# Sliding-window attention with a SwiGLU layer: RMS norm's small steps as tensor_scalar, and a new order table for five engines

## The chip, the cores and the metric

The kernel runs on one core of one Trainium2 chip. The metric is device microseconds for one execution of the whole program. The core has TensorE (PE, matmul, with a separate row PEld for weight loads), VectorE (DVE), ScalarE (ACT), GpSimd (POOL) and SyncE (SP). Plain loads and DMA transposes are issued from SP, loads that cast f32 to bf16 from GpSimd; both run on the same 16 DMA engines.

## What is computed

Attention with a sliding window of 128 and 4 sink keys, then RMS norm and a SwiGLU feed-forward layer, without bias:

```python
# q, k, v: batch 4, heads 8, sequence 768, head_dim 64, f32
scores = q @ k.T / sqrt(64)
keep = (key < 4) | ((0 <= query - key) & (query - key < 128))
a = softmax(where(keep, scores, -1e9))
x = (a @ v) laid out as 3072 tokens x 512
xn = x / sqrt(mean(x * x) + 1e-6) * rms_g
g, val = xn @ w_gate, xn @ w_val          # 512 x 1536 each
out = (g * sigmoid(g) * val) @ w_out      # 1536 x 512, f32 out
```

## The kernel before

The 3072 tokens are 24 blocks of 128 (g = 0 to 23; six blocks are one batch entry), and six groups of four blocks (G = 0 to 5) for the feed-forward part. Per block of attention: q and k are transposed so that head_dim lies on the partitions, by TensorE with a copy by VectorE or ScalarE for blocks 0 to 7 (`pe_t`, `copy_t`), by DMA transposes in SP's queue from block 8 on (`dma_t`). TensorE forms the scores, two heads at a time, with the keys on the partitions; ScalarE takes the exponential into `e`; the masking multiplies or selects `e`: by a bias matmul on TensorE for blocks 0 and 1 (`mask_bias`), by VectorE up to block 15, by GpSimd's affine_select from block 16 on (`tri_pool`, four per block, and `mask_pool_last`, two for the last block of a batch entry). TensorE then forms e times v (`av`, with a column of ones in v that gives the denominator), VectorE divides (`normal`), ScalarE sums the squares (`square`), and VectorE computes the reciprocal root and scales (`rms`).

`rms` is the function that the change edits. It has two tensor_scalar on 128x1 (m, the mean square plus 1e-6; y, a first guess of the reciprocal root from the bits), four scalar_tensor_tensor on 128x1 that refine it (r), and one scalar_tensor_tensor on 128x512 that multiplies x by it and by the gain (xr). xr is then transposed to xnt, by TensorE for blocks 0 to 7 and by DMA in SP's queue from block 8 on.

Per group of the feed-forward part, TensorE multiplies xnt by w_gate and w_val, in pieces whose token width is 128 in group 0, 256 in groups 1 and 2 and 512 after that (g and v, L991); ScalarE takes tanh (th), VectorE makes the silu (p) and the product (hT), TensorE multiplies hT by w_out (o, L1024), ScalarE scales the result to osb and SP stores it.

The kernel first only records its pieces of work with what each needs and gives (`plan.op`; the helpers `dve`, `act`, `pool`, `sp` and `pe` do that). Their order is written out by hand: `ORDER` lists, for each of the five engines, the numbers of the pieces in the order in which this engine does them, counted as they were recorded. Every engine works through its list strictly in order; a piece waits until what it needs is there. `Plan.run` merges the five lists into one program by a small timing model (durations, a DMA model, eight PSUM banks), and the model chooses the banks. Some pieces may run on VectorE or ScalarE; the list in which the number stands decides.

Numbers that matter here: 14, 16 and 18 are the first loads of SP (block 0's k and q as f32, and `grow`, the row of RMS gains); 15 and 17 cast them to bf16; 140 and 138 are the transposes of that k and q on TensorE, 141 and 139 their copies; 20 to 105 are GpSimd's loads, among them 104 (k of block 23) and 105 (v of block 23); 445 to 569 in GpSimd's list are the masks; 564 is the DMA transpose of k of block 23, and 468, 484 and 508 are those of xr of blocks 17, 18 and 19. 106 to 135 are 30 small matmuls on zeros that fill TensorE's time at the start.

GpSimd's loads share one queue. From the ninth on, each load also waits for the landing of the one eight before it.

Of the kernel before, what the change touches and what calls it, by code (L numbers as in the profile page):

```python
# [9 lines left out]
ALU = mybir.AluOpType  # L10
# [24 lines left out]
class Plan:  # L35
# [43 lines left out]
    def run(self, table):  # L79
# [5 lines left out]
        for o in self.ops:  # L85
            for t in o["needs"]:
                users.setdefault(t, []).append(o)
        mode, order = 0, []
        while len(order) < len(self.ops):
            first = None  # L90
            for e in self.START:
                if at[e] == len(ids[e]):
                    continue
                o = self.ops[ids[e][at[e]]]
                k = len(o["takes"])
                if wait[o["at"]] or k > len(self.banks):
                    continue
                ready = o["ready"] + self.HOP[e] if o["ready"] else 0
                if k:
                    ready = max(ready, sorted(self.banks.values())[k - 1] + 40)  # L100
                if o["ring"] == "POOL" and len(last) >= self.DEPTH:
                    ready = max(ready, last[-self.DEPTH])
                start = max(free[e], ready)
                if first is None or start < first[0]:
                    first = start, e, o
            if first is None:
                raise RuntimeError("stuck")
            start, e, o = first
            at[e] += 1
            ns, lat, fn = o["ways"][e]  # L110
            if e == "PE":
                cold = max(0, self.WARM_AT - start)
                ns += min(ns, cold / 2)
                if o["mode"] != mode:
                    ns, mode = ns + 95, o["mode"]
                lat = ns + 180
            for s in o["takes"]:
                i = min(self.banks, key=lambda i: (self.banks[i], i))
                del self.banks[i]
                self.held[s] = i  # L120
            free[e] = start + ns
            end = start + lat
            if o["ring"] is not None:
                end = self.land(o["ring"], end, o["work"]) + self.LATE
                if o["ring"] == "POOL":
                    last.append(end)
            for s in o["drops"]:
                self.banks[self.held[s]] = end + 12
            for t in o["gives"]:
                for x in users.pop(t, ()):  # L130
                    x["ready"] = max(x["ready"], end + 12)
                    wait[x["at"]].discard(t)
            order.append((start, end, e, fn, o))
# [2 lines left out]

ORDER = {
    "PE": """
111 121 124 118 109 135 142 106 140 119 138 134 113 170 108 143 148 136 155 153 129 193
120 172 132 128 162 174 164 175 180 212 195 125 185 117 126 187 115 110 159 122 197 116  # L140
577 166 107 112 131 578 191 204 130 114 133 206 592 597 582 214 593 127 210 583 612 607
587 598 602 588 231 603 216 608 613 617 223 249 225 233 618 235 168 637 647 251 642 229
253 243 632 627 241 260 622 638 266 258 639 633 268 628 294 623 270 643 296 247 644 648
298 264 277 652 279 649 653 662 657 286 288 306 304 654 283 658 672 314 290 667 123 677
663 668 329 678 322 310 682 697 673 344 320 692 683 337 687 335 707 292 359 698 693 717
688 718 350 719 373 352 722 702 366 364 723 712 395 708 703 380 713 382 724 732 727 388
733 728 737 403 742 747 401 729 743 738 734 390 752 748 757 762 753 410 797 758 763 782
425 798 416 418 787 440 777 799 431 772 433 773 767 778 792 768 449 451 788 802 783 803
471 812 804 793 807 813 464 486 808 462 814 480 809 478 822 493 837 823 827 817 838 828
852 842 818 488 502 504 832 847 833 853 843 867 857 848 511 858 872 862 529 873 877 887  # L150
522 863 888 520 878 868 902 540 879 538 889 547 897 903 898 565 937 912 907 913 922 927
908 558 556 892 932 570 882 917 883 918 572 928 923 884 952 942 957 962 947 933 893 943
894 948 938 958 953 977 963 992 959 1002 964 987 997 978 1007 993 982 967 998 983 972
1008 988 968 1012 969 1017 1022 1003 1018 1023 1027 1013 1042 1047 1032 973 1037 1033
1028 974 1038 1048 1043 1039 1049 1044 1052 1055
""",
    "ACT": """
19 15 141 144 146 149 147 145 137 151 150 152 157 173 194 176 178 177 179 181 183 184
182 189 198 200 199 167 201 579 192 208 584 215 211 594 599 589 609 614 232 604 217 219
218 220 619 250 234 227 236-239 252 169 254 256 634 245 624 267 629 640 262 295 273 271  # L160
272 274 297 645 299-302 281 664 650 659 284 308 655 315 316 674 669 317 318 291 330 331
679 332 684 333 345 346 694 347 324 348 699 293 360 689 339 362 709 374 376 720 377 704
354 375 396 397 714 398 399 368 725 739 744 384 749 730 735 759 754 405 764 392 411-414
426-429 420 441 442 779 443 444 774 769 789 784 794 800 435 453 458 460 474 472 473 475
805 466 482 494 495 824 810 496 829 497 819 815 839 834 844 854 849 869 859 506 512-515
530 490 864 531 532 874 533 524 880 904 542 548 890 549-551 899 566 568 909 914 929 924
560 919 934 944 939 574 885 949 954 960 965 979 994 989 984 895 999 1009 1004 1019 1014
1029 1024 970 1034 1040 975 1050 1045 1053 1054
""",
    "DVE": """  # L170
7 0 1 10 2 3 11 12 6 17 139 171 13 156 154 163 158 213 165 196 186 188 160 161 190 4 202
203 205 207 580 209 585 581 586 595 596 600 590 601 610 591 615 605 606 611 221 222 224
226 620 621 228 240 230 616 244 255 257 635 242 261 246 259 630 636 269 625 631 263 275
626 248 276 278 265 280 285 303 282 307 305 287 660 289 665 661 309 670 675 319 671 666
311 323 680 685 681 334 321 676 695 686 338 349 336 325 361 690 696 691 700 351 710 701
363 340 353 705 365 379 378 367 355 715 706 369 389 400 716 711 383 387 740 381 745 385
404 5 402 391 750 746 741 751 760 755 756 406 765 415 761 766 417 419 430 421 432 434
775 776 780 770 781 790 771 452 450 785 795 791 786 436 454 476 796 465 477 463 481 487
479 467 825 485 826 483 830 840 831 841 820 821 503 505 835 489 845 836 855 856 846 850
870 860 861 851 507 875 865 866 521 523 876 871 541 539 525 905 900 901 906 910 543 915  # L180
911 916 559 557 930 571 920 921 925 573 561 931 935 926 940 575 936 945 950 941 955 946
956 951 980 981 995 990 996 985 986 1000 1001 1010 991 1005 1011 1006 1020 1015 1021
1016 1030 1035 1025 1026 1036 1031 1056
""",
    "POOL": """
8 9 20 22 26 21 23 25 29 27 24 32 33 28 36 34 30 35 37 38 42 40 43 41 39 44 31 48 45 47
46 49-53 55 56 58 59 54 57 60-98 445 99 446 447 100 101 459 448 461 102 501 498 103 499
500 516 517 104 518 534 519 536 535 567 537 552 555 105 553 554 569
""",
    "SP": """  # L190
14 18 16 312 327 313 328 646 342 357 343 358 371 641 393 372 394 408 326 656 409 438 341
456 424 651 423 457 439 721 356 370 492 386 491 726 470 469 407 509 422 731 510 437 528
736 801 545 546 484 527 563 468 455 811 508 806 564 544 881 526 562 886 891 576 816 896
971 966 961 1041 976 1046 1051 1057
""",
}

# [2 lines left out]
def kernel(  # L200
# [13 lines left out]
    nc = tc.nc  # L214
# [471 lines left out]
    def rms(g):  # L686
# [7 lines left out]
            scalar2=float(0x5f3759df), op0=ALU.mult, op1=ALU.add,  # L694
        )
        r = small.tile([P, 4], FP32, name="r")
        for o, i0, s, i1, op0 in (
            (0, y, y, m, ALU.mult), (1, r[:, 0:1], -T1, y, ALU.add),
            (2, r[:, 0:1], TP, r[:, 0:1], ALU.add), (3, r[:, 2:3], TQ, r[:, 1:2], ALU.add),
        ):  # L700
            nc.vector.scalar_tensor_tensor(  # L701
                out=r[:, o:o + 1], in0=i0, scalar=s, in1=i1, op0=op0, op1=ALU.mult,
            )
        T["xr", g] = xpool.tile([P, DM], BF16, name="xr")
        nc.vector.scalar_tensor_tensor(  # L705
# [147 lines left out]
    def tri_block(g):  # L853
# [26 lines left out]
        else:  # L880
            for i in range(4):
                pool(590, lambda i=i: tri_pool(g, i), xs + ([("e", g, 0)] if i in (1, 2) else []),
                     [("e", g, i)], g)
            es = [[("e", g, 1), ("e", g, 2)], [("e", g, 0), ("e", g, 3)]]
        T["es", g, 0] = T["es", g, 1] = es

    for g in range(NB):
# [21 lines left out]
        if t + 1 == NT:  # L909
# [8 lines left out]
            for hi in range(2):  # L918
# [5 lines left out]
                        [("e", g, hi)], early)  # L924
                else:
                    pool(590, lambda g=g, hi=hi: mask_pool_last(g, hi), [("x", g, hi)],
                         [("e", g, hi)], g)
                xs.append(("e", g, hi))
            T["xs", g] = [("x", g, 1)]
            T["es", g, 0] = T["es", g, 1] = [xs]  # L930
# [4 lines left out]
        for u in range(2):  # L935
# [12 lines left out]
            early)  # L948
        dve(1745, lambda g=g: rms(g),
            [("ms", g), "gb"] + ([("xt", g - 3)] if g >= 3 else [])  # L950
            + ([("xr", g - 1)] if g else []), [("xr", g)], early)

        G = g // GB
        old = [("F", G - 3, i) for i in range(FTN)] if G >= 3 else []
# [199 lines left out]
```

## Time and profile before

| | |
|---|---|
| median of 3 runs | 245.61 us (244.94 to 246.11) |
| the profiled execution | 246.75 us |
| its span in the profile | 245.0 us |
| TensorE busy | 234.8 us (96%) |
| VectorE busy | 188.3 us (77%) |
| ScalarE busy | 119.4 us (49%) |
| GpSimd busy | 89.7 us (37%) |
| GpSimd's loads | 81760 packets, 13.90 MB |

Times in the profile count from the span's start. A timeline row gives start, duration, engine, line, operation, the tiles written and read, their shapes, how often, and in brackets how long the engine stood idle before it and what ended that. A row of the busy times by stretch gives, after the stretch and its length, the busy microseconds and counts of TensorE, its weight loads, VectorE, ScalarE and GpSimd, then the clock share, the DMA share and GB/s. A row of the waits says which engine and line waited for what, for how long in total, how often, and the longest. Matmuls are pipelined, so a matmul's duration is longer than its distance to the next one.

### The profile page before, as it was taken

The numbers are of one execution on the slowest core, as the hardware profiler recorded it, in microseconds if no ns is written. First come the engines' busy times: TensorE is split into PE (matmuls) and PEld (weight loads), VectorE is DVE, ScalarE is ACT, GpSimd is POOL, SyncE is SP. The second block draws the span as 40 slices with busy tenths as digits, with TensorE's granted clock in tenths as the row PEclk, the third lists the DMA queues.
The fourth block names the chain that finished last, engine by engine and source line by source line (L and its number), as shares of the span: only waits on it lengthen the run. The fifth ranks groups of instructions, "written<-read, shape, count | busy, mean of one in ns | idle before, by whom it ended". The sixth has DMA issues, their size and how long they took to land.

```text
span 245.0 us, 5818 instructions
## 1 busy us (share of the span) xinstructions
PE 234.8 (96%) x2298; PEld 150.5 (61%) x2324; DVE 188.3 (77%) x486; ACT 119.4 (49%) x263; POOL 89.7 (37%) x116
## 2 busy tenths in 40 slices
PE   5899999999999999999999999999989999999994
PEld 2467998875788767687795544445445444444443
DVE  2369889998999999999999889977677853674610
ACT  4377558568575646136765282652732311422221
POOL 8986775679344520039063123052250000000000
PEclk9999999999999999999999999999999999999999
DMA  8999999999999999929995906342033140010305
GB/s 114 164 187 189 181 188 190 153 127 141 149 143 167 128 171 139 207 42 132 199 133 76 190 3 88 86 45 66 3 28 79 21 152 0 0 43 0 131 3 211
DMA packets 113580, 27.38 MB, mean 112 GB/s; under 512 B 103697, under 2 KB 110609, under 8 KB 113554
## 3 DMA queue, kind: packets, MB, share of 16 engines
q0 software_dynamic: 81760, 13.90, 82.6%
q1 hardware_dynamic: 31650, 12.99, 28.4%
q8 instruction: 18, 0.29, 0.5%
q10 hardware_dynamic: 144, 0.13, 0.2%
q14 instruction: 8, 0.07, 0.1%
HBM read 28.31 MB, written 6.29 MB: 141 GB/s over the span
## 4 chain that ended last, share of the span: by engine, by line
PE 83%; DVE 10%; DMA 2%; issue 2%; ACT 1%; SPq 0%
PE v L991 23%; PE o L1024 22%; PE g L991 22%; PE s L601 2%; PE av L659 2%; DMA stage<-in_q_dram 2%; DVE r L701 2%; PE s L523 2%; PE av L654 2%; PE av L644 1%; DVE xr L705 1%; DVE x L673 1%; PE q L483 1%; PE o_last L1042 1%; PE gb L466 1%
## 5 line engine op out<-in xcount | busy, mean ns | idle before, releaser
L991 PE MATMUL v<-xnt,wv 128*128 128x128 bf16 (+2 forms) x525 | 71.6, 282 | 0.4 <-DVE x L673 0.2
L991 PE MATMUL g<-xnt,wg 128*128 128x128 bf16 (+2 forms) x522 | 70.9, 281 | 0.6 <-DVE hT L1014 0.2
L1024 PE MATMUL o<-wo,hT 128*128 128x512 bf16 x259 | 65.4, 379 | 1.8 <-DVE p L1004 0.8
L998 ACT ACTIVATE th<-g 128x512 bf16<-128x512 f32 x72 | 41.1, 600 | 47.3 <-PE g L991 46.6
L1004 DVE SCALAR_TENSOR_TENSOR p<-th,g 128x512 bf16<-128x512 bf16 x72 | 48.0, 681 | 14.3 <-ACT th L998 13.9
L1014 DVE TENSOR_TENSOR hT<-p,v 128x512 bf16<-128x512 bf16 x72 | 47.8, 682 | 11.3 <-PE v L991 10.3
L991 PEld LDWEIGHTS <-wv 128*128 128x128 bf16 x528 | 43.3, 98 | 20.5 <-issue 0.4
L991 PEld LDWEIGHTS <-wg 128*128 128x128 bf16 x528 | 42.8, 98 | 19.6 <-issue 0.5
L1024 PEld LDWEIGHTS <-hT 128*128 128x128 bf16 x276 | 25.4, 98 | 26.8 <-issue 1.5
L395 POOL DMA_DIRECT2D v<-in_v_dram x24 | 21.4, 893 | 28.6 <-DVE rden L672 19.0
L610 ACT ACTIVATE e<-s 128x384 bf16<-128x384 f32 x52 | 22.6, 495 | 8.1 <-PE s L601 6.4
L681 ACT ACTIVATE sq<-x 128x512 bf16<-128x512 bf16 x24 | 15.1, 631 | 19.4 <-DVE x L673 17.9
L1032 ACT ACTIVATE osb<-o 128x512 f32<-128x512 f32 x23 | 13.6, 601 | 22.4 <-PE o L1024 22.3
L391 POOL DMA_DIRECT2D k<-in_k_dram x23 | 20.6, 896 | 10.0 <-DMA v<-in_v_dram 4.0
L635 POOL TENSOR_SCALAR_AFFINE_SELECT e<-e 128x512 bf16<-128x512 bf16 x20 | 13.2, 684 | 28.9 <-ACT e L610 28.8
L391 POOL DMA_DIRECT2D q<-in_q_dram x23 | 20.6, 897 | 4.9 <-DMA k<-in_k_dram 4.6
L673 DVE TENSOR_TENSOR x<-av,rden 128x256 bf16<-128x256 f32 x48 | 20.4, 424 | 1.7
L574 ACT ACTIVATE e<-s 128x512 bf16<-128x512 f32 (+1 forms) x36 | 15.4, 514 | 10.1 <-PE s L523 6.0
L705 DVE SCALAR_TENSOR_TENSOR xr<-x,r,gb 128x512 bf16<-128x512 bf16 x24 | 19.1, 796 | 0.9
L659 PE MATMUL av<-v,e 128*128 128x65 bf16 x192 | 17.2, 195 | 0.2 <-DVE e L585 0.2
L659 PEld LDWEIGHTS <-e 128*128 128x128 bf16 x192 | 13.1, 99 | 3.7 <-ACT e L574 1.7
L654 PE MATMUL av<-v,e 128*128 128x65 bf16 x160 | 14.9, 193 | 0.2
(78 smaller groups left out, 200.8 us busy)
## 6 DMA issues: line engine op xcount, KB each, us to landing
out_dram<-osb SPq DMA_DIRECT2D x23, 256.0 KB, 2.6
v<-in_v_dram POOLq DMA_DIRECT2D x24, 128.0 KB, 8.0
q<-in_q_dram POOLq DMA_DIRECT2D x23, 128.0 KB, 8.2
k<-in_k_dram POOLq DMA_DIRECT2D x23, 128.0 KB, 9.2
wo<-in_moe_w_out_dram POOLq DMA_DIRECT2D x2, 768.0 KB, 10.9
wg<-in_moe_w_gate_dram POOLq DMA_DIRECT2D x5, 256.0 KB, 7.6
wv<-in_moe_w_val_dram POOLq DMA_DIRECT2D x5, 256.0 KB, 9.1
stage<-in_k_dram SPq DMA_DIRECT2D x1, 256.0 KB, 3.1
```

What stands on the lines that cost most here:

```text
L391: nc.gpsimd.dma_start(out=T[name, g], in_=block_of(src, g))
L395: nc.gpsimd.dma_start(out=V16[b][:, t, :, 0:D], in_=block_of(v, g))
L610: nc.scalar.activation(out=e_tile(g)[:, x:x + 2, 0:TW], in_=BANK.pop(("s", g, u, hi))[:, 0:2 * TW].rearrange("p (j c) -> p j c", c=TW), fu ...
L654: nc.tensor.matmul(out=dest, lhsT=T["e", g - 1][:, x, P:2 * P], rhs=V16[b][:, t - 1, h, :], start=(t == 1), stop=False, skip_group_check=True,
L659: nc.tensor.matmul(out=dest, lhsT=T["e", g][:, x, 0:P], rhs=V16[b][:, t, h, :], start=(t == 0), stop=True, skip_group_check=True,)
L673: nc.vector.tensor_tensor(out=T["x16", g][:, 4 * u:4 * u + 4, :], in0=pvv[:, :, 0:D], in1=rden.unsqueeze(2).to_broadcast((P, 4, D)), op=AL ...
L705: nc.vector.scalar_tensor_tensor(out=T["xr", g], in0=T.pop(("x16", g)).rearrange("p h d -> p (h d)"), scalar=r[:, 3:4], in1=gb, op0=ALU.mu ...
L991: nc.tensor.matmul(out=ps[:, i * n:(i + 1) * n], lhsT=w_sb[:, kt, ft * P:(ft + 1) * P], rhs=T["xnt", G][:, kt, cols], start=(kt == 0), sto ...
L998: nc.scalar.activation(out=T["th", key], in_=BANK[("g", key)], func=ACT.Tanh, scale=0.5,)
L1004: nc.vector.scalar_tensor_tensor(out=T["p1", key], in0=T.pop(("th", key)), scalar=1.0, in1=BANK.pop(("g", key)), op0=ALU.add, op1=ALU.mult,)
L1014: nc.vector.tensor_tensor(out=T[hk][:, i:i + n, cols], in0=T.pop(("p1", key)).rearrange("p (n c) -> p n c", n=n), in1=BANK.pop(("v", key)) ...
L1024: nc.tensor.matmul(out=BANK[("o", G, tb)], lhsT=T["h", G, ft // 4][:, ft % 4, tb * P:(tb + 1) * P], rhs=wo[:, ft, :], start=(ft == 0), sto ...
```

## The change

1. In `rms` the four refining steps are issued as tensor_scalar with two scalars instead of scalar_tensor_tensor. The arithmetic is the same; the second tensor operand becomes a second scalar, which is one value per partition.
2. `Plan.run` gets a model of VectorE's `rms` and GpSimd's masks holding each other up (mode 9). It changes no instruction by itself; it only affects how the five lists are merged.
3. `ORDER` is a new table. SP's list begins with k, q, `grow` (14 16 18) instead of k, `grow`, q. GpSimd loads k of block 1 second instead of fourth, and the first weights of the gate eighth instead of fifth. The copies of block 0's k and q change places: k's is now VectorE's, q's ScalarE's; the copy of block 2's k, and those of xr of blocks 4, 5 and 7, move from VectorE to ScalarE. Of the 30 filling matmuls 12 instead of 6 come before the first bias matmuls. GpSimd's masks and its last loads, SP's transposes and stores, and TensorE's feed-forward pieces come in another order. GpSimd's loads up to number 99 (before: 98) stand ahead of its first mask.

The core of the diff; of the three longest lists only the first rows are shown, and all of GpSimd's and SP's:

```diff
@@ -86,6 +86,7 @@
             for t in o["needs"]:
                 users.setdefault(t, []).append(o)
         mode, order = 0, []
+        lock, pool_end = (0, 0), 0
         while len(order) < len(self.ops):
             first = None
             for e in self.START:
@@ -114,6 +115,14 @@
                 if o["mode"] != mode:
                     ns, mode = ns + 95, o["mode"]
                 lat = ns + 180
+            if o["mode"] == 9:
+                if e == "DVE":
+                    more = max(0, pool_end - (start + ns - 770))
+                    lock = start + ns + more - 770, start + ns + more
+                else:
+                    more = lock[1] - start if start < lock[1] and start + ns > lock[0] else 0
+                    pool_end = start + ns + more
+                ns, lat = ns + more, lat + more
             for s in o["takes"]:
                 i = min(self.banks, key=lambda i: (self.banks[i], i))
                 del self.banks[i]
...
 ORDER = {
 "PE": """
-111 121 124 118 109 135 142 106 140 119 138 134 113 170 108 143 148 136 155 153 129 193
-120 172 132 128 162 174 164 175 180 212 195 125 185 117 126 187 115 110 159 122 197 116
...
+111 133 115 121 110 114 120 127 132 131 118 112 142 126 140 138 124 106 170 143 148 136
+162 155 172 153 174 193 212 175 164 180 107 125 109 185 195 187 119 113 129 134 159 122
...
 """,
 "ACT": """
-19 15 141 144 146 149 147 145 137 151 150 152 157 173 194 176 178 177 179 181 183 184
...
+19 15 139 144 146 149 145 147 150 137 151 173 152 157 194 176 178 177 183 179 181 196
...
 """,
 "DVE": """
-7 0 1 10 2 3 11 12 6 17 139 171 13 156 154 163 158 213 165 196 186 188 160 161 190 4 202
-203 205 207 580 209 585 581 586 595 596 600 590 601 610 591 615 605 606 611 221 222 224
...
+7 0-2 11 10 17 6 141 12 171 4 13 163 156 154 158 165 213 5 186 188 160 161 190 202 203
+205 207 580 209 581 585 586 595 600 596 601 610 3 590 591 615 605 606 611 221 222 224
...
 """,
 "POOL": """
-8 9 20 22 26 21 23 25 29 27 24 32 33 28 36 34 30 35 37 38 42 40 43 41 39 44 31 48 45 47
-46 49-53 55 56 58 59 54 57 60-98 445 99 446 447 100 101 459 448 461 102 501 498 103 499
-500 516 517 104 518 534 519 536 535 567 537 552 555 105 553 554 569
+8 9 20-22 26 27 29 25 23 24 32 33 28 34 36 30 35 37 40 39 42 38 43 41 44 31 48 45 47 46
+49-53 55 56 58 59 54 57 60-99 448 100 445-447 101 459 461 102 498 103 499 500 104 519
+501 516 518 537 517 534 536 535 552 554 555 553 567 569 105
 """,
 "SP": """
-14 18 16 312 327 313 328 646 342 357 343 358 371 641 393 372 394 408 326 656 409 438 341
-456 424 651 423 457 439 721 356 370 492 386 491 726 470 469 407 509 422 731 510 437 528
-736 801 545 546 484 527 563 468 455 811 508 806 564 544 881 526 562 886 891 576 816 896
-971 966 961 1041 976 1046 1051 1057
+14 16 18 312 313 327 328 342 357 343 372 358 393 371 646 394 408 641 438 326 341 423 651
+356 456 439 409 656 370 424 470 726 457 386 407 509 721 491 469 422 492 736 731 545 528
+437 527 455 510 811 563 484 546 564 468 801 508 881 806 526 544 562 891 576 816 961 896
+971 976 886 966 1041 1051 1046 1057
 """,
 }
...
@@ -694,12 +703,12 @@
             scalar2=float(0x5f3759df), op0=ALU.mult, op1=ALU.add,
         )
         r = small.tile([P, 4], FP32, name="r")
-        for o, i0, s, i1, op0 in (
+        for o, i0, s0, s1, op0 in (
             (0, y, y, m, ALU.mult), (1, r[:, 0:1], -T1, y, ALU.add),
             (2, r[:, 0:1], TP, r[:, 0:1], ALU.add), (3, r[:, 2:3], TQ, r[:, 1:2], ALU.add),
         ):
-            nc.vector.scalar_tensor_tensor(
-                out=r[:, o:o + 1], in0=i0, scalar=s, in1=i1, op0=op0, op1=ALU.mult,
+            nc.vector.tensor_scalar(
+                out=r[:, o:o + 1], in0=i0, scalar1=s0, scalar2=s1, op0=op0, op1=ALU.mult,
             )
         T["xr", g] = xpool.tile([P, DM], BF16, name="xr")
         nc.vector.scalar_tensor_tensor(
@@ -880,7 +889,7 @@
         else:
             for i in range(4):
                 pool(590, lambda i=i: tri_pool(g, i), xs + ([("e", g, 0)] if i in (1, 2) else []),
-                     [("e", g, i)], g)
+                     [("e", g, i)], g, mode=9)
             es = [[("e", g, 1), ("e", g, 2)], [("e", g, 0), ("e", g, 3)]]
         T["es", g, 0] = T["es", g, 1] = es
 
@@ -924,7 +933,7 @@
                         [("e", g, hi)], early)
                 else:
                     pool(590, lambda g=g, hi=hi: mask_pool_last(g, hi), [("x", g, hi)],
-                         [("e", g, hi)], g)
+                         [("e", g, hi)], g, mode=9)
                 xs.append(("e", g, hi))
             T["xs", g] = [("x", g, 1)]
             T["es", g, 0] = T["es", g, 1] = [xs]
@@ -948,7 +957,7 @@
             early)
         dve(1745, lambda g=g: rms(g),
             [("ms", g), "gb"] + ([("xt", g - 3)] if g >= 3 else [])
-            + ([("xr", g - 1)] if g else []), [("xr", g)], early)
+            + ([("xr", g - 1)] if g else []), [("xr", g)], early, mode=9)
 
         G = g // GB
         old = [("F", G - 3, i) for i in range(FTN)] if G >= 3 else []
```

## Prediction

> **What bounds the kernel now.** I read the page's totals first, then the busy time of each engine by stretch, then who waits for whom on TensorE, then the timeline at the places that these name.
>
> ```profile
> PE 234.8 (96%) x2298; PEld 150.5 (61%) x2324; DVE 188.3 (77%) x486; ACT 119.4 (49%) x263; POOL 89.7 (37%) x116
> ```
>
> ```profile
> 0.00:10.00 10.00, 6.18 (x44) 3.82 (x45) 3.96 (x17) 2.97 (x5) 8.98 (x16) 1.00 1.32 134
> ...
> 140.00:160.00 20.00, 19.65 (x152) 9.41 (x154) 18.36 (x44) 10.90 (x24) 3.74 (x6) 1.00 0.36 66
> ...
> 180.00:200.00 20.00, 19.14 (x117) 9.42 (x118) 16.06 (x41) 6.16 (x13) 1.24 (x3) 1.00 0.38 85
> ...
> 220.00:245.00 25.00, 21.59 (x111) 10.80 (x111) 7.77 (x13) 5.81 (x11) 0.00 (x0) 1.00 0.23 85
> ```
>
> The third number is TensorE's busy time. TensorE is the bound: in the chain that ended last, four 512-column matmuls take 0.86 us in the feed-forward part, start after start, and it has hardly a gap from 25 us to the last matmul at 241.7. So only time in which it starves, or runs slowly, can be won: the first 20 us (3.8 us without work by 10 us), 0.35 us in 140 to 160, 0.86 us in 180 to 200. The 3.4 us at the end are the last output row leaving, which the change doesn't touch.
>
> ```profile
> PE q L483 <- DVE q L387: 2.0, 1, 2.0
> ...
> PE o L1024 <- DVE p L1004: 0.8, 1, 0.8
> ...
> PE g L991 <- DVE hT L1014: 0.2, 1, 0.2
> ```
>
> These waits, of TensorE alone, are the places: the first q block (at 7.35), and two waits for VectorE (182.96 and 150.66).
>
> **The first loads.** The change puts q's load second on the sync queue, where the RMS gain row (`grow`) stood.
>
> ```profile
> 0.81 0.45 SPq L383 DMA_DIRECT2D stage<-in_k_dram  x1
> ...
> 1.32 0.46 SPq L409 DMA_DIRECT2D grow<-in_moe_rms_g_dram  x1
> ...
> 1.83 0.40 SPq L383 DMA_DIRECT2D stage<-in_q_dram  x1
> ...
> 3.95 0.62 ACT L387 CAST k<-stage 128x512 bf16<-128x512 f32 x1 [1.86 <-DMA stage<-in_k_dram]
> ...
> 6.44 0.85 DVE L387 CAST q<-stage 128x512 bf16<-128x512 f32 x1 [3.12 <-DMA stage<-in_q_dram]
> ```
>
> k lands 3.1 us after its issue, q 4.58 us after (at 6.41). By half microseconds:
>
> ```profile
> 2.50:3.00 0.50, 0.39 (x1) 0.13 (x2) 0.46 (x4) 0.00 (x0) 0.50 (x2) 1.00 1.21 275
> ...
> 3.50:4.00 0.50, 0.50 (x3) 0.23 (x2) 0.00 (x0) 0.05 (x1) 0.50 (x2) 1.00 0.46 107
> ...
> 4.50:5.00 0.50, 0.48 (x5) 0.38 (x5) 0.00 (x0) 0.07 (x1) 0.50 (x2) 1.00 1.62 191
> ```
>
> The last number is GB/s: 275 while k streams, 107 in the hole between k's end and q's start, and then GpSimd's loads take their share. Issued 0.51 us sooner, q gains 0.51 at least. At most it follows k at 275 GB/s: 64 KB by 2.5 (128 GB/s in that half microsecond), 137 KB each half microsecond after, 476 of 524 KB by 4.0, the rest by 4.3, and 0.5 us to landing (k's bytes end near 3.4, it lands at 3.9): 4.8. I take 5.0, nearest to k's row: 1.4 us sooner. Not all arrives. Behind q's cast (0.87, to 5.87) VectorE now has the memset of `ones` (0.17), k's copy (0.42) and the masks (0.65 to 0.75), until 7.2; q's copy moves to ScalarE (0.59 for 0.42). Block 1's q is still a GpSimd load, landed 5.2 us after its issue at 1.76, at 6.96: transposes to 7.6, copy to 8.0. Before, that copy ended at 9.05 and the first scores 0.67 later. So block 0's scores gain 1.0 us. `grow` lands later, but its matmul stands behind these scores (9.65).
>
> From there to 24 us the same work follows, and can run 1.0 us sooner. But until about 16.9 us TensorE runs at half speed: four 512-column mask matmuls took 1.71 us at 13.77, twice the 0.86 above. If full speed comes at the same moment as before, up to half of the microsecond is lost again; if it comes sooner, because the work is denser sooner, half of the 3.1 us from 13.8 to 16.9 may run at twice the speed, 0.8 more, 1.8 in all. I take 0.9, range 0.3 (0.51 less the 0.17 of the slower copy) to 1.8. The Trainium skill (TensorE: Matmul & The Clock Gate, Part 1) says that the array gets its full clock after one busy window of about 3.4 us, and that the windows run freely; an estimate by it, with one window less at half speed, would be 1.7 us less on work that only TensorE limits, while the profile's clock column shows 1.00 throughout.
>
> The table also reorders GpSimd's first loads (k1 third to second place, the first gate weights fourth to eighth). The tightest weight piece in 20 to 35 us landed 2.9 us before its first matmul (30.5 against 33.3, from the landings in the trace), which covers 0.9 us. At a gain of 1.8, 1.1 would be left.
>
> **The norm's small steps.** Per block two tensor_scalar and four scalar_tensor_tensor on 128x1, then `xr`; the four become tensor_scalar, the counts stay.
>
> ```profile
> 133.79 0.14 DVE L688 TENSOR_SCALAR m<-ms 128x1 f32<-128x1 f32 x1
> 133.97 0.15 DVE L692 TENSOR_SCALAR y<-m 128x1 int32<-128x1 int32 x1
> 134.15 0.24 DVE L701 SCALAR_TENSOR_TENSOR r<-y,m 128x1 f32<-128x1 f32 x1
> 134.43 0.56 DVE L701 SCALAR_TENSOR_TENSOR r<-r,y 128x1 f32<-128x1 f32 x1
> ...
> 179.69 0.99 DVE L701 SCALAR_TENSOR_TENSOR r<-y,m 128x1 f32<-128x1 f32 x1
> 180.72 0.55 DVE L701 SCALAR_TENSOR_TENSOR r<-r,y 128x1 f32<-128x1 f32 x1
> ```
>
> GpSimd ran affine_selects on `e` from 133.28 to 134.97 and 179.43 to 181.2. Under them the steps with two tensor inputs stretch (0.22 to 0.99, 0.16 to 0.56), those with one don't (0.14, 0.15). From `m` to `xr` the plain case takes 1.08 us, the four disturbed ones 1.49 (133.8), 1.93 (145.1), 1.45 (160.7) and 2.24 (179.3): 2.8 us in all, and `xr` itself (0.75) lost 1.1 more in three blocks. On the path are two. At 179 the 1.16 us delay `xr`, then `p` (182.23 to 182.91), for which TensorE's o waits: 0.92 us beyond the normal step between matmuls. Without it p ends at 181.75, before the last av at 182.04, and nothing waits; next late is g's own order. At 145 the small steps lose 0.85 and `xr` 0.46, and hT at 149.3 keeps TensorE 0.36 us. Both go: 1.28 us; the new order places everything anew, so I take 1.2, range 0.4 to 1.3.
>
> The Trainium skill (SBUF — State Buffer, Who interferes with whom) says that tensor_scalar can itself enter a two-port mode and then blocks against GpSimd, which speaks against this change. The rows of `m` and `y` under a select disagree at this size. By that rule the steps' share would stay and about 1 us of the sum with it.
>
> **What tensor_scalar costs.** It now reads one or two [128,1] scalars from memory, which `m` and `y` don't. Nearest row: among the four steps the one with such a scalar takes 0.219 us, those with a constant 0.153 to 0.160. Without that cost the four gain 0.07 us per block, with it each loses up to 0.06, 0.24 in all; I take 0.1, 2.4 us over 24 blocks. VectorE has 8.1 idle us between 40 and 160 (111.87 busy of 120), so most hides: 0.2 us on the path, range -0.1 to 1.0.
>
> **What the new table puts at risk.** The sync queue goes strictly in order, and transposes issued during load bursts land 8 to 9 us after issue (range over k and q: 2.5 to 9.4). In the new order k12's transpose stands ahead of k11's and q13's ahead of q12's, each behind a GpSimd load. With the loads where they landed before (k12 70.1, q13 74.8), k11 lands at 80.0 and q12 at 84.7, 0.5 to 0.9 us before their scores if TensorE runs 1.4 us sooner; x9, 0.8 us early before, is as tight at 99.5. So gains beyond about 1.5 us at the start run into these. v23, now behind the last selects, keeps 2 to 3 us (2.4 before). I charge 0.2, range 0 to 1.0.
>
> **Sum.** -0.9 - 1.2 + 0.2 + 0.2 = -1.7 us, against the profiled execution's 246.75 (span 245.0): 245.05. That execution lies 1.14 above the median of the runs shown; on the median, 245.61, it gives 243.9.
>
> **Rivals.** (a) The start gains more, full speed coming sooner: -1.8 for -0.9, so 243.0, or 242.6 with nothing lost by the last two terms; for it speaks the denser start, against it the transposes above. (b) The start's gain is given back at 80 to 100 us: the 0.9 is lost, the other terms stay: 244.8. For it: landings that loads pace, not TensorE. (c) The change doesn't do what it says, the small steps stay disturbed: 1.0 of the 1.2 is lost: 244.9. (d) Slower: k23's transpose now stands in the sync queue ahead of x17's and x19's. It needs k23's load, which GpSimd issued at 161.15 before, behind selects. In the new order that load stands behind block 19's selects (145 to 149), and all is well. If it is held up as before, k23 lands at 164.5, x17 and x19 land at 168.3 and 170.2, and the fifth token group (about 166) waits 2.3 to 4.2 us; it decides from a landing after about 160. That is 246.2 to 248.1, 247.2 in the middle.
>
> **Numbers.** Forecast 0.54, (a) 0.11, (b) 0.16, (c) 0.09, (d) 0.10. Range 242.4 to 245.7: from just under (a) to (b) and (c) with the ends of the two unknown costs (0.8 more); (d) and the tails lie outside. A difference of 0.5%, 1.2 us, is about what a measurement of this kernel tells from none. Faster (below 244.38): nine tenths of the forecast, (a), and a little of (b) and (c): 0.62. Within 0.5%: 0.28. Slower: 0.10.
>
> **What would show it.** Right: q's cast starts at 5.0 to 5.9, the first o matmul of 182 follows without a wait, no step on 128x1 exceeds 0.3 us, and 80 to 100 shows no new TensorE wait. Wrong: steps of 0.4 us and more, a wait of TensorE for a transpose, or SP held by k23 near 152.

## The result, and the profile after

| | before | after |
|---|---|---|
| median | 245.54 us (7 runs, 244.94 to 246.11) | 243.51 us (7 runs, 242.75 to 244.02) |
| ratio after to before | | 0.9916, 95% interval 0.9896 to 0.9935 |
| the profiled execution | 246.75 us | 242.75 us |
| its span | 245.0 us | 241.0 us |

The change makes the kernel 2.0 us faster. The two profiled executions lie 4.0 us apart, because that of before was longer than all seven other runs and that of after was the shortest of its seven.

First the page's totals and its row of the granted clock, then the busy time by stretch (TensorE's is the third number, the clock share the third from the end).

```profile
PE 235.0 (98%) x2324; PEld 149.8 (62%) x2324; DVE 187.0 (78%) x482; ACT 122.3 (51%) x267; POOL 89.9 (37%) x116
...
PEclk9679999999999999999999999999999999999999
```

```profile
0.00:10.00 10.00, 7.73 (x61) 4.42 (x61) 3.46 (x19) 4.94 (x11) 8.97 (x16) 0.91 1.53 135
10.00:20.00 10.00, 9.76 (x120) 6.81 (x119) 7.84 (x29) 7.89 (x22) 8.00 (x11) 0.75 1.53 177
...
140.00:160.00 20.00, 20.00 (x148) 9.43 (x139) 19.28 (x43) 10.90 (x23) 4.24 (x7) 1.00 0.45 73
...
180.00:200.00 20.00, 20.00 (x117) 9.59 (x116) 16.25 (x42) 4.96 (x11) 0.00 (x0) 1.00 0.25 52
```

TensorE's gaps of 140 to 160 and of 180 to 200 are gone; of the first 10 us it works 7.7 instead of 6.2. (The trace of before lacks 26 of the 2324 matmuls, so a part of its small gaps is only missing records. The waits below don't suffer from that.) All of TensorE's waits that the view still lists:

```profile
PE warm L468 <- DVE zeros L335: 1.1, 1, 1.1
PE q L492 <- DVE q L396: 0.6, 1, 0.6
PE k L492 <- ACT k L396: 0.4, 1, 0.4
```

All three lie in the first 6 us. The waits for p and hT at 183 and 151 are no longer there, and nothing new stands between 80 and 100 us. The timeline at the start shows the first loads:

```profile
1.32 0.57 SPq L392 DMA_DIRECT2D stage<-in_q_dram  x1
...
4.74 0.40 PE L492 MATMUL k<-ident,k 128*128 128x128 bf16 x4 [0.41 <-ACT k L396]
5.26 0.43 DVE L396 CAST q<-stage 128x512 bf16<-128x512 f32 x1 [3.29 <-DMA stage<-in_q_dram]
...
10.11 1.90 PE L514 MATMUL s<-bias,ident 128*128 128x512 bf16 x4
```

q lands 3.9 us after its issue, 1.2 us sooner than before. The hole in the transfer rate is gone; the same half microsecond that had 107 GB/s now has 265 (the last number):

```profile
3.50:4.00 0.50, 0.50 (x2) 0.15 (x1) 0.00 (x0) 0.00 (x0) 0.50 (x2) 1.00 1.32 265
```

And the norm under GpSimd's selects, here one after another on VectorE and GpSimd:

```profile
130.98 1.55 POOL L573 TENSOR_SCALAR_AFFINE_SELECT e<-e 128x512 bf16<-128x512 bf16 x2 [6.51 <-ACT e L559]
...
131.74 0.27 DVE L710 TENSOR_SCALAR r<-y,m 128x1 f32<-128x1 f32 x1
132.05 0.21 DVE L710 TENSOR_SCALAR r<-r,y 128x1 f32<-128x1 f32 x1
```

Both steps run inside the selects (130.98 to 132.53) and take what they take elsewhere. No step on 128x1 exceeds 0.275 us in the whole trace, and `xr` is lengthened by 0.02 us in all 24 blocks together (before: 1.1).

**Where the time came from.** The two tables put TensorE's pieces in another order, so equal moments can't be compared. I compare equal amounts of work instead: the columns that TensorE's pieces move, at 2.4 per ns (a 512-column matmul then counts 0.213 us), fillers left out, summed along each kernel's own list. The table gives the moment (us) at which so much useful work was begun, interpolated between the starts of pieces, in one profiled execution of each kernel; "end" is the start of the last output piece. The kernels are those of the experiments.

| kernel | 7 us of work | 19 | 97 | 137 | 177 | end | 137 to 177 |
|---|---|---|---|---|---|---|---|
| before | 19.47 | 33.09 | 108.07 | 145.02 | 184.41 | 240.12 | 39.39 |
| e1, tensor_scalar | 18.67 | 32.37 | 107.99 | 145.00 | 183.39 | 239.09 | 38.39 |
| e9, the same from block 16 | 17.84 | 31.52 | 106.46 | 143.42 | 181.79 | 237.49 | 38.37 |
| e2, q second | 17.91 | 31.62 | 106.26 | 143.22 | 182.61 | 238.32 | 39.39 |
| e10, three parts | 15.97 | 30.45 | 105.35 | 142.31 | 180.68 | 236.38 | 38.37 |
| after | 17.38 | 30.39 | 105.49 | 142.44 | 180.40 | 236.13 | 37.96 |
| e12, the same again | 17.74 | 30.88 | 106.08 | 143.03 | 180.99 | 236.72 | 37.96 |
| e11, after with the old steps | 17.98 | 31.58 | 106.49 | 143.44 | 181.40 | 237.13 | 37.96 |
| e6, after with 6 fillers | 18.80 | 31.67 | 106.74 | 143.69 | 181.65 | 237.38 | 37.96 |
| e7, e11 with fillers in holes | 15.73 | 30.78 | 106.11 | 143.07 | 181.03 | 236.76 | 37.96 |

Two places decide. Between 137 and 177 us of work (the norms of the last blocks), every kernel with the new table gains 1.43 us over before, every one with tensor_scalar in the old table 1.0. The rest is set before 19 us of work, and there even two executions of one kernel differ: after and e12 by 0.5 us, e11 and e3, which is the same kernel (30.63), by 0.95. The loads make these differences. First some rows of the chain of work that ended last in the changed kernel (start, duration, what), then a wait of e8, the same kernel again:

```profile
14.14 9.69 DMA wv<-in_moe_w_val_dram
24.13 7.73 DMA q<-in_q_dram
...
32.30 0.89 PE v L1000 x16
```

```profile
29.20 1.96 PE L1000 MATMUL g<-xnt,wg 128*128 128x128 bf16 x32 [0.23 <-DMA wg<-in_moe_w_gate_dram]
```

The chain runs through GpSimd's load queue until 31.9 us; in before it ran through block 0's q load and then through the engines' own work. The last early piece of w_gate lands at 28.84 us in after, 29.07 in e3, 29.23 in e7, 29.32 in e12 and 30.03 in e11. In each, TensorE's weight loads wait for it (0.16 to 0.95 us), and 19 us of work are reached 1.55 to 1.56 us after it lands. In e6 it lands at 29.43, and TensorE, late itself, doesn't wait.

### The profile page after: what moved, and what is told of

It reads as the page before. It is cut to its first block, busy times and chain, and to the rows that moved or that the text cites. A ratio compares the mean times of both kernels' runs of the same rounds, so it can differ in the third digit from the quotient of the medians.

```text
span 241.0 us, 5846 instructions
## 1 busy us (share of the span) xinstructions
PE 235.0 (98%) x2324; PEld 149.8 (62%) x2324; DVE 187.0 (78%) x482; ACT 122.3 (51%) x267; POOL 89.9 (37%) x116
## 4 chain that ended last, share of the span: by engine, by line
PE 85%; DMA 7%; POOL 5%; issue 0%; DVE 0%; POOLq 0%
PE o L1033 25%; PE v L1000 24%; PE g L1000 23%; DMA wv<-in_moe_w_val_dram 4%; DMA q<-in_q_dram 3%; PE s L610 3%; PE av L668 2%; PE av L663 2%; PE av L653 2%; POOL wg L446 1%; POOL q L400 1%; POOL v L404 1%; PE o_last L1051 1%; POOL k L400 1%; PE s L532 1%; POOL wv L446 1%
## 5 line engine op out<-in xcount | busy, mean ns | idle before, releaser
L1000 PE MATMUL v<-xnt,wv 128*128 128x128 bf16 (+2 forms) x528 | 73.3, 282 | 0.0
L1033 PE MATMUL o<-wo,hT 128*128 128x512 bf16 x276 | 67.7, 379 | 0.0
L1007 ACT ACTIVATE th<-g 128x512 bf16<-128x512 f32 x72 | 41.6, 600 | 45.0 <-PE g L1000 40.0
L1013 DVE SCALAR_TENSOR_TENSOR p<-th,g 128x512 bf16<-128x512 bf16 x72 | 47.5, 682 | 17.6 <-ACT th L1007 17.4
L1000 PEld LDWEIGHTS <-wv 128*128 128x128 bf16 x528 | 42.7, 98 | 19.9 <-issue 0.7
L644 POOL TENSOR_SCALAR_AFFINE_SELECT e<-e 128x512 bf16<-128x512 bf16 x20 | 12.6, 652 | 51.1 <-ACT e L619 50.8
L690 ACT ACTIVATE sq<-x 128x512 bf16<-128x512 bf16 x24 | 15.3, 636 | 17.9 <-DVE x L682 17.7
L714 DVE SCALAR_TENSOR_TENSOR xr<-x,r,gb 128x512 bf16<-128x512 bf16 x24 | 18.0, 752 | 0.8
L668 PE MATMUL av<-v,e 128*128 128x65 bf16 x192 | 17.8, 196 | 0.2
L583 ACT ACTIVATE e<-s 128x512 bf16<-128x512 f32 (+1 forms) x36 | 16.0, 528 | 2.8 <-PE s L532 2.3
L663 PE MATMUL av<-v,e 128*128 128x65 bf16 x160 | 15.5, 193 | 0.0
```

The costliest lines, as they stand in the source:

```text
L663: nc.tensor.matmul(out=dest, lhsT=T["e", g - 1][:, x, P:2 * P], rhs=V16[b][:, t - 1, h, :], start=(t == 1), stop=False, skip_group_check=True,
L668: nc.tensor.matmul(out=dest, lhsT=T["e", g][:, x, 0:P], rhs=V16[b][:, t, h, :], start=(t == 0), stop=True, skip_group_check=True,)
L714: nc.vector.scalar_tensor_tensor(out=T["xr", g], in0=T.pop(("x16", g)).rearrange("p h d -> p (h d)"), scalar=r[:, 3:4], in1=gb, op0=ALU.mu ...
L1000: nc.tensor.matmul(out=ps[:, i * n:(i + 1) * n], lhsT=w_sb[:, kt, ft * P:(ft + 1) * P], rhs=T["xnt", G][:, kt, cols], start=(kt == 0), sto ...
L1007: nc.scalar.activation(out=T["th", key], in_=BANK[("g", key)], func=ACT.Tanh, scale=0.5,)
L1013: nc.vector.scalar_tensor_tensor(out=T["p1", key], in0=T.pop(("th", key)), scalar=1.0, in1=BANK.pop(("g", key)), op0=ALU.add, op1=ALU.mult,)
```

## The experiments

Each time is set against runs of the kernel before on the same chip. Medians in us; a ratio stands with its 95% interval.

| run | median | ratio to before |
|---|---|---|
| e1 tensor_scalar alone | 245.35 | 1.001 (0.9993 to 1.0027) |
| e2 q second alone | 244.88 | 0.998 (0.9964 to 0.9996) |
| e3 after, old steps | 242.86 | 0.991 (0.9888 to 0.9932) |
| e4 after, `grow` second | 243.38 | 0.994 (0.9915 to 0.9966) |
| e5 before, 12 fillers early | 244.81 | 0.9983 (0.9963 to 1.0003) |
| e6 after, 6 fillers early | 243.52 | 0.9917 (0.9893 to 0.994) |
| e7 after, old steps, fillers in holes | 243.37 | 0.9907 (0.9884 to 0.993) |
| e8 after | 243.23 | 0.9905 (0.9882 to 0.9928) |
| e9 tensor_scalar from block 16 alone | 244.54 | 0.9957 (0.9942 to 0.9971) |
| e10 q second, 12 fillers, e9's steps | 243.49 | 0.992 (0.9896 to 0.9943) |
| e11 e3 again | 242.94 | 0.9895 (0.9869 to 0.9921) |
| e12 after | 243.23 | 0.9907 (0.9883 to 0.993) |

**e1: tensor_scalar alone, in the old table.**

```diff
-            nc.vector.scalar_tensor_tensor(
-                out=r[:, o:o + 1], in0=i0, scalar=s, in1=i1, op0=op0, op1=ALU.mult,
+            nc.vector.tensor_scalar(
+                out=r[:, o:o + 1], in0=i0, scalar1=s0, scalar2=s1, op0=op0, op1=ALU.mult,
```

> The kernel before with the four small norm steps as tensor_scalar and nothing else. Theory (start and norm steps both count): the two TensorE waits of 0.36 us near 150 and 0.92 us near 182 go, the pointer scalars add 0.24 us per block of which little shows: 1.0 us faster than before, about 244.5. Rival (the whole gain comes from the new start of the table): the stretched steps were hidden and the longer steps cost: 0 to 0.5 us slower than before.

No gain: 1.001. The theory's 244.5 was missed; the rival's time came (by the ratio), but not its reason, as the stretched steps were not hidden. The timeline of e1 says why. The first group is GpSimd's selects and VectorE's steps and `xr` of one late block; then come a TensorE wait at 101.6 and, last, the o that follows that `xr`.

```profile
178.92 1.23 POOL L635 TENSOR_SCALAR_AFFINE_SELECT e<-e 128x512 bf16<-128x512 bf16 x2
...
179.62 0.45 DVE L701 TENSOR_SCALAR r<-r 128x1 f32<-128x1 f32 x2
...
180.11 1.18 DVE L705 SCALAR_TENSOR_TENSOR xr<-x,r,gb 128x512 bf16<-128x512 bf16 x1
```

```profile
101.63 0.27 PE L991 MATMUL g<-xnt,wg 128*128 128x256 bf16 x1 [0.21 <-DVE hT L1014]
```

```profile
181.93 0.38 PE L1024 MATMUL o<-wo,hT 128*128 128x512 bf16 x1 [0.24 <-DVE p L1004]
```

The steps are free of the selects, but `xr`, which still has two inputs of 128x512, now meets the select that the steps met before: 1.18 instead of 0.75 us. Over all blocks `xr` lost 1.4 us, 0.3 more than before. Still the steps win 1.0 us between 137 and 177 us of work; TensorE's wait for p falls from 0.76 to 0.24. What eats it lies elsewhere. A step with such a scalar costs 54 ns more than the scalar_tensor_tensor did (r<-y,m 0.273 for 0.219), so `m` to `xr` takes 1.30 for 1.08 us in every block. In blocks 7 to 13 VectorE is busy 96% of the time (60 to 100 us), and there e1 lost against before what it had gained at the start: TensorE waits for hT at 101.6.

**e9: tensor_scalar only where GpSimd masks.**

```diff
+            if g < 16:
+                nc.vector.scalar_tensor_tensor(...)      # as before
+            else:
+                nc.vector.tensor_scalar(...)             # as in e1
```

> The kernel before with one edit: the four refining steps are tensor_scalar only from block 16 on, where GpSimd does the masking; blocks 0 to 15 keep scalar_tensor_tensor. Theory V (e1 lost in blocks 7 to 13, through VectorE's longer steps, what it won after block 16): the losses near 90 to 102 us vanish, the win after 140 us stays, time 0.8 to 1.0 us under before, ratio 0.9955 to 0.9975. Rival W (the steps' stretch is only moved to xr, so tensor_scalar wins nothing wherever it stands; e1's profile was flattered by its start): ratio 0.9985 to 1.001.

0.9957 (1.06 us, interval 0.71 to 1.42): theory V. From 19 to 97 us of work e9 takes 74.94 us and e1 75.62, the 0.7 us that the dearer steps of blocks 0 to 15 cost in the old table; from 137 to 177 both take the same 38.4. The ratios of e1 and e9 lie 1.3 us apart, the medians 0.8. What of that lies beyond the 0.7, if anything, isn't located.

**e3 and e11: the new table with the old steps.** The diff is e1's, reversed, in the changed kernel.

> The changed kernel with the four small steps as scalar_tensor_tensor again. Theory (tensor_scalar is needed against GpSimd's selects): some blocks from 18 on are stretched again, and 0.5 to 1.0 us is lost against the changed kernel: 244.0 to 244.5. Rival (the new order alone keeps the selects away from the norm): no stretched step, each block's norm 0.2 us shorter, equal to the changed kernel or up to 0.3 faster: 243.2 to 243.5.

> The same kernel as e3 (the changed one with scalar_tensor_tensor again), beside the changed one on one chip. If tensor_scalar is needed in the new table, it is slower than e12 by 0.3 us or more; if the new table alone keeps masks and norm apart, it is equal to or up to 0.4 us faster than e12, since each block's steps are 0.2 us shorter.

Nothing is lost: 242.86 and 242.94, against 243.51, 243.23 and 243.23 of the changed kernel (result, e8 and e12). In e3's trace one single step is lengthened, at the place whose rows of the changed kernel are shown above:

```profile
131.42 1.34 POOL L573 TENSOR_SCALAR_AFFINE_SELECT e<-e 128x512 bf16<-128x512 bf16 x2 [6.60 <-ACT e L559]
...
132.22 0.55 DVE L710 SCALAR_TENSOR_TENSOR r<-r,y 128x1 f32<-128x1 f32 x1
```

0.55 with two tensor inputs and 0.21 with a scalar in its place, both under two selects. The small steps of the other norms lie where GpSimd doesn't mask (in the changed kernel the last ones begin at 140.4, 157.3, 174.9 and 179.8; the selects near them lie at 142.9, 159.4, 172.5 to 175.0 and 176.5 to 178.0). So the table alone removes nearly all of the contention. Nor does tensor_scalar cost anything there: from 19 us of work to the end after takes 205.74 us, e12 205.84 and e11 205.55. Whether the old steps are a little faster (0.3 to 0.6 us between the medians) the intervals don't settle.

> The changed kernel without any edit, for a comparison on this chip with the other runs of this call. By the result so far: ratio to before 0.990 to 0.9935. If scalar_tensor_tensor in the new order (e3, 0.991) is as good as tensor_scalar, this ratio lies within 0.0015 of it; if tensor_scalar costs 0.2 us or more there, this ratio is 0.992 to 0.994.

> The changed kernel without any edit, beside e11: ratio to before 0.990 to 0.9935 as in the result.

Both repeat the result.

**e2 and e4: which load is second in SP's list.** e2 gives the old table the new order, e4 gives the new table the old one:

```diff
-14 18 16 312 327 313 328 ...
+14 16 18 312 327 313 328 ...
```

> The kernel before with q's load ahead of grow in the sync queue (14 16 18) and nothing else. Theory: q's cast starts near 5.3 instead of 6.44, block 0's scores end about 1 us sooner, and 0.9 us of it stays: 244.6. Rival (the start only pays together with the 12 filling matmuls ahead of the first bias matmuls, which bring TensorE to full speed sooner): less than 0.4 us, 245.1 or more.

> The changed kernel with grow second in the sync queue again (14 18 16). Theory: q's cast starts 0.5 to 1.2 us later, and 0.9 us is lost against the changed kernel: 244.4. Rival (GpSimd's loads near 32 us set the pace after the start, whatever the start does): less than 0.3 us lost, 243.5 to 243.8.

e2 gains 0.5 us (0.1 to 0.9), between its theory and its rival. In the new table the reverse edit gives 0.994 against 0.9905 to 0.9916, some 0.7 us, though the intervals overlap; by the medians (243.38 against 243.23 to 243.51) it costs nothing. So what q is worth in the new table isn't resolved. In e4's profile block 0's q transposes start at 6.75 instead of 5.74 us.

**e5 and e6: how many fillers stand ahead of the first bias matmuls.** e5 moves six more to the front in the old table, e6 takes six away from it in the new one:

```diff
-111 121 124 118 109 135 142 ...
+111 121 124 118 109 135 130 114 133 127 123 131 142 ...
```

> The kernel before with one edit: six more of the 30 filling matmuls (130 114 133 127 123 131) stand ahead of the first bias matmuls, 12 instead of 6, as in the changed kernel; SP still loads grow second. Theory F (the fillers start TensorE's full speed early: in the changed kernel's profile the transposes of k at 4.74 run at 0.40 us for four, in before's at 0.61): k's transposes take 0.40 us, full speed is lost again near 9 us and comes back near 15 us instead of 16.9, and the time is 0.5 to 1.0 us under before, ratio 0.996 to 0.998. Rival Q (the start is paced by the landing of q alone; when full speed comes makes no difference because the data for block 0 are late anyway): the first feed-forward matmul stays at 19.1 to 19.9 us, ratio 0.9985 to 1.0015.

> The changed kernel with one edit: six of the twelve early filling matmuls (120 127 132 131 118 112) go back behind block 0's scores, so that 6 stand ahead of the first bias matmuls as before. Theory F: k's transposes at half speed (0.61 us for four), no stretch of full speed before 9 us, full speed from about 16 us; the time lies 0.5 to 1.0 us above the changed kernel's, ratio to before 0.994 to 0.996. Rival Q: no difference, ratio to before 0.990 to 0.9925 as the changed kernel's 0.9916.

On the median, neither is told from no change (0.9983 with an interval that holds 1; 0.9917 beside 0.9905 and 0.9907), as rival Q had it. But the fillers do something, in about half of the executions. In the profile after, TensorE's k transposes at 4.74 take 0.40 us, full speed, and the four bias matmuls at 10.11 take 1.90, half speed again; the clock row reads 9, 6, 7, 9. In e8, the same kernel, the k transposes took 0.61 and the clock row shows nothing. A mean granted clock under 0.995, which in the profiles marks an early full speed that was lost again, came in 29 of 62 executions of kernels with 12 early fillers and in 1 of 98 with 6. In e5 the six executions with it took 244.62 us on the mean, the six without it 245.28. In the six kernels with the new table, twelve fillers and no further ones (after, e3, e4, e8, e11, e12) the same split gives 0.0 to 0.8 us, 0.4 on the mean. The loads that hold TensorE there would be a reason for less; that it is less isn't resolved.

**e7: keep the full speed.** e3's kernel, with ten later fillers moved into TensorE's two holes before k's and q's transposes:

```diff
-... 142 126 140 138 124 106 170 ...
+... 142 126 119 113 129 134 140 122 108 135 123 130 116 138 124 106 170 ...
```

> The changed kernel with scalar_tensor_tensor again in the norm (as in e3) and ten of the later filling matmuls moved into the two holes of TensorE that its profile shows, four into 4.3 to 4.7 (before k's transposes) and six into 5.1 to 5.7 (before q's). Theory F: with the holes filled the granted full speed is kept past 9 us, block 1's four bias matmuls take 0.9 instead of 1.9 us and the first feed-forward matmul comes 0.5 to 1.2 us sooner; the part of it that GpSimd's loads do not give back at 31.9 us, 0.2 to 0.6 us, shows in the time: ratio 0.987 to 0.990. Rival L (the loads of GpSimd limit from 20 to 32 us): the first feed-forward matmul comes sooner but the time stays, ratio 0.9900 to 0.9920. Rival S (the full speed is lost in any case at about 9 us): bias matmuls of block 1 stay at 1.9 us, ratio 0.9900 to 0.9920.

The mechanism works up to 17.7 us, and the time stays. The page's clock row of e7 and three rows of its timeline:

```profile
PEclk9997999999999999999999999999999999999999
```

```profile
9.57 1.11 PE L514 MATMUL s<-bias,ident 128*128 128x512 bf16 x4
...
17.50 0.93 PE L1000 MATMUL g<-xnt,wg 128*128 128x128 bf16 x8 [0.40 <-DMA wg<-in_moe_w_gate_dram]
18.22 1.92 PE L1000 MATMUL v<-xnt,wv 128*128 128x128 bf16 x16
```

The clock is full from 4.0 us on, the bias matmuls of block 1 take 1.11 instead of 1.90, and the feed-forward part starts at 16.48 instead of 17.84. But TensorE has waited 1.05 us for VectorE just before (at 16.25), waits 0.40 for a piece of w_gate at 17.50, and from 17.7 to 21.1 us the clock is at half again: it is the fourth digit of the row, and the v piece at 18.22 takes 1.92 us, 1.06 in after. Half speed for 3.4 us costs, as an estimate, up to 1.7 us of TensorE's work, more than the 1.36 that were won. By 19 us of work e7 is at 30.78, where the kernel without the edit is (30.63 in e3, 31.58 in e11). So this execution alone doesn't tell the loads' part from the clock's. For rival L speak the loads themselves: the last early piece of w_gate lands at 29.23 us, as in the other kernels, and TensorE waits for it again. The other five executions, none of them profiled, had a mean clock of 1.00 and took 242.58 to 243.58 us. Without any further fillers, e11 has the longest of these waits:

```profile
30.07 1.96 PE L1000 MATMUL g<-xnt,wg 128*128 128x128 bf16 x32 [0.78 <-DMA wg<-in_moe_w_gate_dram]
```

The DMA engines move 171 to 178 GB/s from 5 to 32 us in before, after, e7 and e10, whatever TensorE does.

**e10: three parts, and the old table otherwise.** e2's, e5's and e9's edits together.

> The kernel before with three edits and no other change of its order table: q's load second in SP's list, six more filling matmuls early (as in e5), tensor_scalar from block 16 on (as in e9). Theory V with the parts adding up: 0.5 for q, 0.2 to 0.4 for the fillers, 0.8 to 1.0 for the steps, 1.5 to 1.9 us under before, ratio 0.992 to 0.994, nearly the whole of the change. Rival T (the rest of the new table carries it, the way masks and norms are placed): ratio 0.996 to 0.998, as q and fillers alone.

0.992 (0.9896 to 0.9943), beside 0.9905 to 0.9916 of the whole change. The three parts alone, 1.06 for the steps, 0.5 for q and up to 0.4 for the fillers, bring nearly all of it; what the rest of the new table adds (at most 0.4 us by these medians) isn't resolved. Its place is seen, though: 37.96 against 38.37 us from 137 to 177 us of work.

No version beats the changed kernel by more than the measurement can tell; e3 is the simplest of the fastest.

## Why the prediction was right, and where not

The forecast case came in: 243.9 predicted, 243.51 measured, well inside the range of 242.4 to 245.7. The terms of its sum fared differently.

**The first loads, -0.9.** Near in size, with one cause mistaken. The medians leave 0.6 us for the start: 2.03 less the 1.43 of the norm steps. q's cast was put at 5.0 and came at 5.26, inside the bounds (the earlier one should read 4.7: at 275 GB/s the last 48 KB end at 4.2, not 4.3). q alone is worth 0.5 us in e2; e4 doesn't settle it for the new table. The prediction had TensorE's half speed last until 16.9 us, or end sooner where the work is denser. But this moment isn't fixed by the work: before, e1 and e9 have the same first loads and fillers, and q's later transposes ran thus in before, e1 and e9:

```profile
16.59 0.61 PE L483 MATMUL q<-ident,q 128*128 128x128 bf16 x4
```

```profile
15.85 0.54 PE L483 MATMUL q<-ident,q 128*128 128x128 bf16 x4
```

```profile
15.17 0.40 PE L483 MATMUL q<-ident,q 128*128 128x128 bf16 x4
```

By the spacing of the matmuls full speed came for good at 17.2, 16.2 and 14.3 us. e1 and e9 stand alike until then, and at 19 us of work they are 0.85 us apart; before is later by another 0.7, most of it q's cast (TensorE waited 2.0 us for it, 1.4 in e1 and e9). So the start of one execution tells that of the next only to within about a microsecond, which goes far to explain profiles 4.0 us apart beside medians 2.0 apart. The Trainium skill (TensorE: Matmul & The Clock Gate, Part 1) has the windows that decide on the clock run freely, not from the kernel's start; the three moments agree with it.

**Its cover, -0.9 against 2.9 us of slack in the weight loads.** This step failed. The landing times were those of the old load order in one late execution, and by them the loads could not become the limit before 2.9 us were gained. In the new order the last early piece of w_gate is the tight one: it lands at 28.84 us in the changed kernel, and TensorE's weight load waits 0.16 us for it. So nothing is left of the cover in the result itself. In e3, e7, e8, e11 and e12 that wait is 0.18 to 0.95 us, in e10 0.25 us at 28; only e4 and e6, of the eight profiles with the new table, don't have it. So something like rival (b), gain given back, did come, but at 29 to 32 us instead of 80 to 100, and it takes what TensorE gains beyond the landings, not the whole 0.9. Rival (a), full speed sooner, also came in about half of the executions, but was worth 0.4 us on the mean in the new table and not its 0.9.

**The norm steps, -1.2.** Right in place and size (1.43 in the new table, just beyond the range's 1.3), wrong in the cause. The prediction had it come from tensor_scalar alone and let `xr` recover with it. e1 and e9 show 1.0 from tensor_scalar, with `xr` still held up; e3 and e11 show the 1.43 from the table with no tensor_scalar at all. The change has two remedies for one wait, and they don't add. The rule of the Trainium skill (SBUF — State Buffer, Who interferes with whom) that spoke against the change, that tensor_scalar can itself block against GpSimd, was not seen on 128x1 in any run (0.275 us at most, with fifteen of the steps under selects in e1). The same section's rule that a VectorE instruction with two SBUF inputs contends with a GpSimd instruction that reads SBUF fits the 0.55 and 0.21 us.

**What tensor_scalar costs, +0.2.** The cost of a block was mis-sized: 0.22 us instead of 0.1, near the bound of 0.24. On the path it is 0.7 us in the old table (e1 against e9), inside the range of -0.1 to 1.0, and nothing that can be seen in the new one. "VectorE's idle time hides most" holds for the whole stretch from 40 to 160 but not for its densest part.

**The new table's risk, +0.2.** Nothing of it came in the changed kernel. No transpose of k11, q12 or x9 was waited for, and k23's did not hold the sync queue, so rival (d) fell. The transpose that is tight is one that the prediction didn't name, block 8's q: it landed about 0.3 us ahead of its use in the changed kernel and held TensorE for 0.28 us at 56.2 in e3.

**Rival (c)** fell: no step is disturbed.

So the total is right partly by luck. The start brought 0.3 us less than its term and the norm 0.2 us more, the latter through the table; and the two charges of 0.2, which didn't come, set the forecast above the measured time.

## What to carry to other kernels

Two parts of one change can remove the same wait; only the experiment with each part alone shows that the sum of their prices would count it twice. An instruction that frees a wait at one end is paid for wherever it runs, so put it only in the blocks that have the wait (e9 against e1: 0.5%, for one `if`). A start that is worked on should first be asked what comes after it: here TensorE waits for the last early gate weights, at 28.8 to 30.0 us, in six of the eight profiles with the new table, and what it gains beyond that is taken back.

## What the runs showed of the hardware

- TensorE's granted clock went back to half after a thin stretch: in the profile after, full speed lasted from 4.8 to 8.2 us and came back at 15.0. With the two holes of together 1.0 us filled (e7), it lasted from 4.0 to 17.7, and was lost until 21.1 after waits of 1.05 and 0.40 us. In the five profiles with an early full speed (after, e3, e5, e7, e10) it lasted 3.4 us, in e7 13.7, and the half speed behind it 3.4 or 6.8 us, so each stretch is 3.4 us or two or four times that.
- The profile's clock share stays at 1.00 in the first half-speed stretch (before: 1.00 throughout, with 0.61 us for four transposes) and falls under 1 only after full speed had been granted once (0.91 and 0.75 after).
- A tensor_scalar on 128x1 with scalars from memory takes 0.273 (two) and 0.21 us (one), against 0.14 to 0.15 with constants, and 54 ns more than the scalar_tensor_tensor that it stands for.
- VectorE's cast of q, 128x512 f32 to bf16, took 0.85 us in before's profile and 0.43 in after's. In eleven of the other twelve profiles it took 0.43, in e7 0.50. What lengthened it is open; no run was made for it.
